# A one-core delta-rule and gated feed-forward kernel: another hand-kept order of all its work, 94 steps given to another engine or taken back, and nine filler products in place of five

## The chip, the cores and the metric

The kernel runs on one core of a Trainium2 chip. The metric is device microseconds of that core for one execution; smaller is better. The names used here are those of the profile: PE is TensorE, DVE is VectorE, ACT is ScalarE, POOL is GpSimd, and SP is SyncE, whose queue issues nearly all DMAs.

## The reference

Two blocks follow each other. The first runs over 768 positions for each of 4 batches and 8 heads; the second takes its output, token by token, through two matrix products with a gate between them.

```python
for t in range(S):                       # B, H, S, D = 4, 8, 768, 48
    kt, vt, bt = (k_n[:, :, t], v[:, :, t], beta[:, :, t, None])
    y[:, :, t] = np.einsum('bhd,bhde->bhe', q[:, :, t], state)
    v_old = np.einsum('bhde,bhd->bhe', state, kt)
    state = state + bt[:, :, :, None] * np.einsum('bhd,bhe->bhde', kt, vt - v_old)
...
h = x @ w_in                             # x: 3072 tokens of 384; w_in 384 x 2048
g = h * np.cos(h)
return (g @ w_out).astype(np.float32)    # w_out 2048 x 384
```

## The kernel before

**The first block** is cut into 24 units of 32 positions, and two units form a pair. For every unit PE forms the products of keys and queries with the keys (`gram`, L625), reads the state (`state`, L834), solves a triangular system by multiplying with an inverse that lies ready (`solve`, L897), updates the state (`update`, L920) and forms the output (`within`, L937; `features`, L956). DVE and ACT carry the results from one of these steps to the next.

**The inverse** of units 0 to 3 is made by row elimination on DVE and POOL (L727, L734, with products at L707). From unit 4 on it is made by POOL for a whole pair at once, and this is the path that the prediction follows. DVE writes the scaled products (`gram_keys`, L639). SP's queue puts them into device memory (`gram_put`, L766) and fetches them in another layout (`gram_get`, L775, tile `gb`). POOL inverts them in seven steps of a few columns each (`inv`, L797 and L804; 62 instructions for a pair). SP's queue puts the result out (`put`, L808) and fetches it for each unit of the pair (`get`, L817, four DMAs, tile `zt`). Only then can `solve` of that unit run. There is one buffer for `gb` and one for the matrix that is being inverted, so `gram_get` of a pair waits for the end of the inverse of the pair before it.

**The second block** works on pairs of units (256 tokens). The first two pairs form their hidden values with plain products (`hidden`, L980), the others with 20 block products and sums in place of 24 (`layer`, L1158; the sums over the inputs are `x_sum`, L1073, and those over the weights `in_sums`, L1116 and L1120). The gate is taken by ACT and DVE (`turns`, `rest`, `cos`, `gate`, L1021 to L1040). The output of the first pair is plain (L1181), that of the others takes seven products of half-size blocks in place of eight (`product`, L1246), with sums over the gated values (`left`, L1262) and over the weights (`right`, L1275), and collecting steps (L1298). The weights arrive in 28 pieces at the start; each is unpacked by ACT (`split`, L497 and L499), DVE (`shift`, L503 and L508) and POOL (`add`, L512).

**The order** is not found by a scheduler when the kernel is built. All work is registered as some 2,150 named steps with what they depend on. `Order.LINE` is a written list of their numbers, and `Order.run` issues them in just that order; each engine then works through its own instructions in this order and never takes a later one first. A step waits for what it depends on, and everything behind it on the same engine waits with it. Some steps may go to either of two engines: those listed in `Order.OTHER` go to the second one (for `left`, `right`, `weigh` and a few others POOL in place of DVE, for `x_sum` DVE in place of POOL, for `fold` and `unfold` ACT in place of DVE).

**Constant products** (`heat`, L1194) multiply a constant by itself into the output bank, and nothing reads the result. They are further work for PE in places where it has little. `HEAT` lists their widths. Before the change there are five, and the first output product (L1181) is registered as depending on all of them.

Of the kernel before, what the change touches and what calls it, by code (L numbers as in the profile page):

```python
# [46 lines left out]
HEAT = (512, 256, 256, 512, 128,)  # L47


class Order:  # L50

    OTHER = {
        ('weigh', 0, 0), ('unfold', 0), ('weigh', 0, 1), ('fold', 1), ('unfold', 1),
        ('weigh', 1, 0), ('fold', 2), ('weigh', 1, 1), ('unfold', 2), ('unfold', 3),
        ('right', 4, 0), ('left', 1, 2, 0), ('x_sum', 2, 'd'), ('x_sum', 2, 'n'),
        ('x_sum', 2, 'm'), ('x_sum', 2, 'e'), ('x_sum', 2, 'k'), ('x_sum', 2, 'g'),
        ('x_sum', 2, 'i'), ('x_sum', 2, 'l'), ('x_sum', 2, 'f'), ('x_sum', 2, 'h'),
        ('x_sum', 2, 'b0'), ('left', 2, 2, 0), ('x_sum', 3, 'd'), ('x_sum', 3, 'n'),
        ('x_sum', 3, 'm'), ('x_sum', 3, 'e'), ('x_sum', 3, 'k'), ('x_sum', 3, 'g'),
        ('x_sum', 3, 'i'), ('x_sum', 3, 'l'), ('x_sum', 3, 'f'), ('x_sum', 3, 'h'),  # L60
        ('x_sum', 3, 'b0'), ('left', 3, 1, 0), ('left', 3, 4, 1), ('left', 3, 3, 0),
        ('x_sum', 4, 'd'), ('x_sum', 4, 'n'), ('x_sum', 4, 'm'), ('x_sum', 4, 'e'),
        ('x_sum', 4, 'k'), ('x_sum', 4, 'g'), ('x_sum', 4, 'l'), ('x_sum', 4, 'f'),
        ('x_sum', 4, 'h'), ('x_sum', 4, 'b0'), ('left', 4, 4, 0), ('left', 4, 3, 0),
        ('left', 4, 3, 1), ('x_sum', 5, 'd'), ('x_sum', 5, 'm'), ('x_sum', 5, 'e'),
        ('x_sum', 5, 'i'), ('x_sum', 5, 'f'), ('x_sum', 5, 'h'), ('left', 5, 2, 0),
        ('left', 5, 4, 0), ('left', 5, 4, 1), ('left', 5, 3, 0), ('x_sum', 6, 'd'),
        ('x_sum', 6, 'e'), ('x_sum', 6, 'l'), ('x_sum', 6, 'f'), ('x_sum', 6, 'h'),
        ('x_sum', 6, 'b0'), ('left', 6, 2, 1), ('left', 6, 4, 0), ('left', 6, 3, 0),
        ('x_sum', 7, 'd'), ('x_sum', 7, 'n'), ('x_sum', 7, 'm'), ('x_sum', 7, 'g'),  # L70
        ('x_sum', 7, 'i'), ('x_sum', 7, 'h'), ('left', 7, 1, 0), ('left', 7, 2, 0),
        ('left', 7, 2, 1), ('left', 7, 4, 0), ('left', 7, 3, 1), ('x_sum', 8, 'd'),
        ('x_sum', 8, 'm'), ('x_sum', 8, 'e'), ('x_sum', 8, 'k'), ('x_sum', 8, 'f'),
        ('x_sum', 8, 'h'), ('x_sum', 8, 'b0'), ('left', 8, 4, 1), ('left', 8, 3, 0),
        ('x_sum', 9, 'n'), ('x_sum', 9, 'e'), ('x_sum', 9, 'k'), ('x_sum', 9, 'i'),
        ('x_sum', 9, 'b0'), ('left', 9, 2, 0), ('left', 9, 1, 1), ('left', 9, 4, 0),
        ('left', 9, 4, 1), ('left', 9, 3, 0), ('left', 9, 3, 1), ('x_sum', 10, 'd'),
        ('x_sum', 10, 'n'), ('x_sum', 10, 'e'), ('x_sum', 10, 'g'), ('x_sum', 10, 'l'),
        ('x_sum', 10, 'f'), ('x_sum', 10, 'h'), ('x_sum', 10, 'b0'), ('left', 10, 1, 0),
        ('left', 10, 1, 1), ('left', 10, 4, 0), ('left', 10, 3, 0), ('x_sum', 11, 'f'),  # L80
        ('x_sum', 11, 'b0'), ('left', 11, 1, 0), ('left', 11, 2, 0), ('left', 11, 2, 1),
        ('left', 11, 4, 0), ('left', 11, 4, 1),
# [139 lines left out]
def kernel(  # L222
# [1084 lines left out]
    def store(p, i, cols=slice(0, DM)):  # L1307
# [12 lines left out]
            x=2, x_sum=XS, turns=2, g=GATES, o=2, o_out=2,  # L1320
# [507 lines left out]
```

## Time and profile before

| what | value |
|---|---|
| three runs | 643.1, 647.96 and 650.33 us, median 647.96 |
| the profiled execution | 644.59 us, with a span of 642.8 us |
| PE | 613.6 us busy (95%) |
| DVE | 505.4 us busy (79%) |
| POOL | 447.9 us busy (70%) |
| ACT | 263.3 us busy (41%) |
| granted TensorE clock, mean | 0.981 |
| DMA | 50.01 MB, mean 78 GB/s |

The span is the time from the first to the last instruction of the program. Busy time counts overlapping instructions of one engine once. A row of the timeline gives start, length, engine, line, operation and, in brackets, how long the engine stood idle ahead of it and what ended that. PE works through its products one behind the other, so that a wait shows only where its whole queue ran dry.

### The profile page before, as it was taken

To read this page: it belongs to the slowest core of one execution; us is meant where nothing else is said; L and a number is where in the kernel's file an instruction comes from. 1 tells how busy PE (TensorE), PEld (TensorE's weight loads), DVE (VectorE), ACT (ScalarE), POOL (GpSimd) and SP (SyncE) were. 2 spreads that over 40 slices of the span, in tenths; PEclk is the share of its full clock that TensorE was granted. 3 is DMA by queue.
4 is the path that set the end of the run, shared out by engine and by line. 5 is a ranking of instruction groups with operands and counts; after the bars stand their busy time and mean duration, and the time that the engine had idled before them with its cause. 6 is when DMAs were issued, how large, how long until landed. Compare 5 with 4: busy or idle time off the path is not lost.

```text
span 642.8 us, 28246 instructions
## 1 busy us (share of the span) xinstructions
PE 613.6 (95%) x12316; PEld 572.7 (89%) x12316; DVE 505.4 (79%) x955; ACT 263.3 (41%) x467; POOL 447.9 (70%) x783
## 2 busy tenths in 40 slices
PE   5677999999999999999998999999999999999997
PEld 4566888886999989999998999999999999999997
DVE  7896887599999888789788778777778867556582
ACT  3535565822233631533523533622633433435340
POOL 4465899888888788787888886885897874152032
PEclk9677999999999999999999999999999999999999
DMA  6884475554453542635535404425304202000000
GB/s 122 217 215 133 102 197 140 123 93 70 75 96 51 100 76 40 115 64 99 89 42 98 86 7 84 74 53 101 67 2 85 51 2 34 28 2 26 2 25 25
DMA packets 202924, 50.01 MB, mean 78 GB/s; under 512 B 194544, under 2 KB 197760, under 8 KB 202800
## 3 DMA queue, kind: packets, MB, share of 16 engines
q1 hardware_dynamic: 201536, 47.82, 37.5%
q8 instruction: 97, 1.59, 1.1%
q10 hardware_dynamic: 1088, 0.20, 0.2%
q0 software_dynamic: 176, 0.18, 0.2%
q14 instruction: 27, 0.22, 0.1%
HBM read 38.19 MB, written 9.96 MB: 75 GB/s over the span
## 4 chain that ended last, share of the span: by engine, by line
PE 87%; DVE 7%; DMA 1%; issue 1%; POOL 1%; ACT 1%; SPq 0%; DVEq 0%; POOLq 0%
PE p_out L1246 29%; PE p_h L1158 28%; PE p_h L980 7%; PE p_kq L834 4%; PE p_out L1181 3%; PE p_u L897 3%; PE p_g L625 3%; PE p_s L920 3%; PE p_kq L937 3%; PE p_o L1246 2%; PE p_z L956 1%; DVE rows L734 1%; PE p_t L594 1%; DVE rows L727 1%; DVE g_ffn L1175 1%
## 5 line engine op out<-in xcount | busy, mean ns | idle before, releaser
L797 POOL TENSOR_TENSOR part<-z,gb 128x126 f32<-128x126 f32 (+22 forms) x310 | 138.8, 448 | 39.9 <-DMA gb<-g_dr 7.9
L804 POOL TENSOR_TENSOR z<-z,part 128x126 f32<-128x126 f32 (+22 forms) x310 | 145.8, 470 | 24.3
L1246 PE MATMUL p_out<-w_out,g_ffn 128*128 128x192 f32 x672 | 121.6, 329 | 2.0 <-DVE o L1298 1.8
L1246 PEld LDWEIGHTS p_out<-w_out,g_ffn 128*128 128x128 f32 x672 | 107.8, 190 | 3.7 <-issue 2.2
L1037 ACT ACTIVATE turns<-turns,halfpi 128x512 f32<-128x512 f32 x96 | 68.4, 720 | 78.7 <-DVE turns L1028 78.3
L1262 POOL TENSOR_TENSOR g_ffn<-g_ffn 128x512 f32<-128x512 f32 x37 | 49.0, 1329 | 67.3 <-DVE g_ffn L1040 46.0
L1246 PE MATMUL p_out<-w_sum,g_ffn 128*128 128x192 f32 x496 | 90.1, 329 | 0.4 <-DVE o L1298 0.4
L1158 PE MATMUL p_h<-x_sum,w_in 128*128 128x128 f32 x640 | 83.0, 277 | 0.3 <-DVE g_ffn L1175 0.3
L1246 PEld LDWEIGHTS p_out<-w_sum,g_ffn 128*128 128x128 f32 x496 | 79.5, 190 | 1.4 <-DVE o L1298 0.6
L1158 PEld LDWEIGHTS p_h<-x_sum,w_in 128*128 128x128 f32 x640 | 77.8, 192 | 1.7 <-DVE g_ffn L1175 0.6
L1021 ACT ACTIVATE turns<-g_ffn,quarter_turn 128x512 int32<-128x512 f32 x70 | 49.2, 719 | 59.8 <-DVE g_ffn L1175 38.9
L1175 DVE TENSOR_TENSOR g_ffn<-g_ffn,p_h 128x512 f32<-128x512 f32 x80 | 54.1, 679 | 24.6 <-PE p_h L1158 23.6
L1028 DVE SCALAR_TENSOR_TENSOR turns<-g_ffn,turns 128x512 f32<-128x512 f32 x70 | 55.8, 805 | 15.1 <-ACT turns L1021 14.9
L1040 DVE TENSOR_TENSOR g_ffn<-turns,g_ffn 128x512 f32<-128x512 f32 x70 | 50.9, 736 | 12.7 <-ACT turns L1037 12.6
L1158 PE MATMUL p_h<-x_sum,in_sum 128*128 128x128 f32 x400 | 54.0, 278 | 0.3 <-issue 0.3
L1158 PEld LDWEIGHTS p_h<-x_sum,in_sum 128*128 128x128 f32 x400 | 49.3, 191 | 1.5 <-issue 0.4
L980 PE MATMUL p_h<-x_ffn,w_in 128*128 128x128 f32 x384 | 48.3, 285 | 0.0
L980 PEld LDWEIGHTS p_h<-x_ffn,w_in 128*128 128x128 f32 x384 | 45.7, 198 | 1.0 <-issue 0.2
L1262 DVE TENSOR_TENSOR g_ffn<-g_ffn 128x512 f32<-128x512 f32 x51 | 44.3, 872 | 1.6 <-PE p_out L1246 1.5
L541 POOL TENSOR_TENSOR knrm<-ksum,halves 128x16 f32<-128x16 f32 (+1 forms) x14 | 38.8, 2768 | 9.0 <-DVE ksum L529 7.9
L1298 DVE SCALAR_TENSOR_TENSOR o<-p_out,o 128x192 f32<-128x192 f32 x74 | 25.0, 350 | 24.5 <-PE p_out L1246 23.8
L1170 ACT COPY p_h<-p_h 128x512 f32<-128x512 f32 x40 | 23.0, 574 | 48.9 <-PE p_h L1158 33.6
(145 smaller groups left out, 1052.9 us busy)
## 6 DMA issues: line engine op xcount, KB each, us to landing
gb<-g_dr SPq DMA_DIRECT2D x20, 256.0 KB, 4.1
vp<-in_v_dram SPq DMA_DIRECT2D x96, 48.0 KB, 3.0
in_sum<-in_moe_w_out_dram SPq DMA_DIRECT2D x12, 384.0 KB, 3.3
out_dram<-o SPq DMA_DIRECT2D x23, 192.0 KB, 2.5
in_sum<-in_moe_w_in_dram SPq DMA_DIRECT2D x8, 512.0 KB, 5.3
kp<-in_k_dram SPq DMA_DIRECT2D x128, 24.0 KB, 2.2
z_dr<-z SPq DMA_DIRECT2D x10, 256.0 KB, 3.6
zt<-z_dr SPq DMA_DIRECT2D x80, 32.0 KB, 2.4
```

The source lines that it names most:

```text
L541: nc.gpsimd.tensor_tensor(out=scales[m][2][:, part], in0=sums[m, part.start][:, 0:n], in1=halves[:, 0:n], op=ALU.pow,)
L797: nc.gpsimd.tensor_tensor(out=part, in0=z[:, 0:rows, j, None].to_broadcast(shape), in1=a[:, j, None, j + 1 :].to_broadcast(shape), op=ALU. ...
L804: nc.gpsimd.tensor_tensor(out=behind, in0=behind, in1=part, op=ALU.subtract)
L980: nc.tensor.matmul(p_h[:, i], w_in[:, t, (4 * k + i) * 128 : (4 * k + i + 1) * 128], xts[p][:, t, unit * 128 : (unit + 1) * 128], start=(i ...
L1021: nc.scalar.activation(turns[p, f], hidden_of(p, f), AF.Identity, bias=quarter_turn, scale=TURN)
L1028: nc.vector.scalar_tensor_tensor(out=r, in0=hidden_of(p, f), scalar=TURN, in1=t, op0=ALU.mult, op1=ALU.subtract,)
L1037: nc.scalar.activation(r, r, AF.Sin, bias=halfpi, scale=2.0 * math.pi)
L1040: nc.vector.tensor_tensor(out=place(p, f), in0=step_of(rests.pop((p, f)), f), in1=step_of(hidden_of(p, f), f), op=ALU.mult,)
L1158: nc.tensor.matmul(p_h[:, e], in_block(*w)[:, e], x_of(p, b), start=new and e == 0, stop=True, skip_group_check=True,)
L1175: nc.vector.tensor_tensor(out=part_of(p, to), in0=part_of(p, one), in1=part_of(p, two), op=op)
L1246: nc.tensor.matmul(p_o, left(p, part, a)[:, e % 4], right(e, b), start=(e == 0), stop=(e == FT // 2 - 1), skip_group_check=True,)
L1262: either(("left", p, x, s), nc.vector, nc.gpsimd).tensor_tensor(out=left(p, s, to), in0=left(p, s, one), in1=left(p, s, two), op=op)
```

## The change

Three things are edited, and nothing that is computed for the output changes.

- `LINE` is another permutation of the same steps, with four numbers more for the new constant products. Every engine's queue has another order, SP's included.
- `OTHER` differs in 94 steps: 25 `left` sums go from POOL to DVE and 16 from DVE to POOL; 22 `x_sum` sums go each way; 3 `weigh` products go from POOL to DVE; 3 `right` sums go from DVE to POOL and 1 back; 1 `fold` goes from DVE to ACT and 1 `unfold` from ACT to DVE.
- `HEAT` has nine widths (2,816 columns in all) in place of five (1,664), and the first output product is no longer registered as depending on them.

```diff
-HEAT = (512, 256, 256, 512, 128,)
+HEAT = (256, 128, 256, 512, 128, 256, 512, 512, 256,)
...
     OTHER = {
-        ('weigh', 0, 0), ('unfold', 0), ('weigh', 0, 1), ('fold', 1), ('unfold', 1),
...
+        ('weigh', 0, 0), ('unfold', 0), ('fold', 1), ('unfold', 1), ('fold', 2), ('fold', 3),
...
     LINE = """
-92 0 1 2 21 15 3 16 9 54 2143 10 11 17 55 18 93 123 2031 124 2035 14 4 60 56 57 6 22 2039 95 23 61
...
+0 15 16 9 1 21 17 2031 2 11 2035 3 2143 2039 22 14 18 54 4 6 7 5 23 55 19 92 56 60 24 25 2032 57
...
                 if last:
                     deps.append(last)
-                else:
-                    deps += [("heat", x) for x in range(len(HEAT))]
```

What the new order does to the queues that the prediction speaks of:

| queue | before | after |
|---|---|---|
| SP, first steps | k and q of units 2 and 3, then weight pieces between them | weight pieces 0 to 2, v of unit 0, k of unit 2, weight piece 3, q of unit 2 |
| DVE, ahead of the first elimination (L727) | no weight piece | weight pieces 0, 1 and 2 |
| PE, ahead of the first `hidden` product | both `gram` of units 2 and 3 | `gram` of unit 2 alone; eight of the nine constant products |
| POOL, inside the inverse of the first pair | weight pieces 14 to 21 | weight pieces 15 to 21 and 24, one `right` |
| SP, at the end of the inverse of units 6 and 7 | `put`, `gram_get`, `get` of unit 6 | `put`, `gram_put` of unit 9, `get` of unit 6, `gram_get` |
| SP, at the end of the inverse of units 16 and 17 | `put`, `gram_get`, `get`, `get` | `put`, `get` of unit 16, `gram_get` |
| SP, at the end of the inverse of units 20 and 21 | `put`, `gram_get`, a load, a store, a load, `get`, `get` | `put`, two `gram_put`, `get`, a store, `get`, `gram_get` |

More of the change, by code (lines that the diff above doesn't have):

```diff
@@ L44, in _consts @@
     ).astype(np.float32)
-HEAT = (512, 256, 256, 512, 128,)
+HEAT = (256, 128, 256, 512, 128, 256, 512, 512, 256,)
 class Order:
     OTHER = {
-        ('weigh', 0, 0), ('unfold', 0), ('weigh', 0, 1), ('fold', 1), ('unfold', 1),
[L54 to L61, printed above, removed]
-        ('x_sum', 4, 'd'), ('x_sum', 4, 'n'), ('x_sum', 4, 'm'), ('x_sum', 4, 'e'),
[L63 to L82, printed above, removed]
@@ new lines @@
+        ('weigh', 0, 0), ('unfold', 0), ('fold', 1), ('unfold', 1), ('fold', 2), ('fold', 3),
+        ('unfold', 2), ('right', 1, 2), ('right', 3, 2), ('right', 3, 6), ('left', 1, 1, 0),
+        ('left', 1, 4, 0), ('left', 1, 4, 1), ('x_sum', 2, 'd'), ('x_sum', 2, 'n'),
+        ('x_sum', 2, 'e'), ('x_sum', 2, 'k'), ('x_sum', 2, 'g'), ('x_sum', 2, 'i'),
+        ('x_sum', 2, 'l'), ('x_sum', 2, 'f'), ('x_sum', 2, 'h'), ('left', 2, 4, 0),
+        ('x_sum', 3, 'd'), ('x_sum', 3, 'n'), ('x_sum', 3, 'm'), ('x_sum', 3, 'e'),
@@ new lines @@
+        ('x_sum', 3, 'k'), ('x_sum', 3, 'g'), ('x_sum', 3, 'i'), ('x_sum', 3, 'l'),
+        ('x_sum', 3, 'f'), ('x_sum', 3, 'h'), ('left', 3, 1, 0), ('left', 3, 3, 1),
+        ('x_sum', 4, 'd'), ('x_sum', 4, 'n'), ('x_sum', 4, 'm'), ('x_sum', 4, 'e'),
+        ('x_sum', 4, 'k'), ('x_sum', 4, 'l'), ('x_sum', 4, 'f'), ('x_sum', 4, 'h'),
+        ('x_sum', 4, 'b0'), ('left', 4, 4, 0), ('x_sum', 5, 'd'), ('x_sum', 5, 'm'),
+        ('x_sum', 5, 'k'), ('x_sum', 5, 'g'), ('x_sum', 5, 'i'), ('x_sum', 5, 'l'),
@@ new lines @@
+        ('x_sum', 5, 'h'), ('x_sum', 5, 'b0'), ('left', 5, 1, 0), ('left', 5, 4, 1),
+        ('left', 5, 3, 1), ('x_sum', 6, 'n'), ('x_sum', 6, 'm'), ('x_sum', 6, 'e'),
+        ('x_sum', 6, 'i'), ('x_sum', 6, 'l'), ('x_sum', 6, 'f'), ('x_sum', 6, 'h'),
+        ('left', 6, 2, 0), ('x_sum', 7, 'd'), ('x_sum', 7, 'e'), ('x_sum', 7, 'i'),
+        ('x_sum', 7, 'f'), ('x_sum', 7, 'h'), ('x_sum', 7, 'b0'), ('left', 7, 1, 0),
+        ('x_sum', 8, 'd'), ('x_sum', 8, 'n'), ('x_sum', 8, 'k'), ('x_sum', 8, 'g'),
@@ new lines @@
+        ('x_sum', 8, 'l'), ('x_sum', 8, 'f'), ('x_sum', 8, 'h'), ('left', 8, 2, 0),
+        ('left', 8, 2, 1), ('left', 8, 3, 0), ('left', 8, 3, 1), ('x_sum', 9, 'm'),
+        ('x_sum', 9, 'l'), ('x_sum', 9, 'h'), ('x_sum', 9, 'b0'), ('left', 9, 1, 1),
+        ('left', 9, 2, 1), ('left', 9, 4, 0), ('left', 9, 3, 1), ('x_sum', 10, 'd'),
+        ('x_sum', 10, 'n'), ('x_sum', 10, 'm'), ('x_sum', 10, 'e'), ('x_sum', 10, 'k'),
+        ('x_sum', 10, 'l'), ('x_sum', 10, 'f'), ('x_sum', 10, 'b0'), ('left', 10, 1, 0),
@@ L83 @@
+        ('left', 10, 4, 1), ('left', 10, 3, 0), ('x_sum', 11, 'n'), ('x_sum', 11, 'k'),
+        ('x_sum', 11, 'i'), ('x_sum', 11, 'h'), ('left', 11, 1, 0), ('left', 11, 1, 1),
+        ('left', 11, 4, 1), ('left', 11, 3, 0), ('left', 11, 3, 1),
     }
     LINE = """
[98 rows of a table removed]
[98 rows of a table added]
 """
```

194 rows, old and new, of the table LINE are left out of this document.

## The prediction

> **What bounds the kernel now.** I read the page first: busy shares, slices and granted clock.
>
> ```profile
> span 642.8 us, 28246 instructions
> ...
> PE 613.6 (95%) x12316; PEld 572.7 (89%) x12316; DVE 505.4 (79%) x955; ACT 263.3 (41%) x467; POOL 447.9 (70%) x783
> ...
> DVE  7896887599999888789788778777778867556582
> ...
> PEclk9677999999999999999999999999999999999999
> ```
>
> PE is busy for 95% of the span and the clock is low only in the first tenth. So I read the busy time by stages (columns: stretch, its length, then PE, PEld, DVE, ACT, POOL; then granted clock, DMA share, GB/s).
>
> ```profile
> 0.00:20.00 20.00, 12.48 (x188) 9.97 (x188) 15.51 (x52) 7.83 (x15) 6.79 (x12) 1.00 0.73 145
> 20.00:60.00 40.00, 28.02 (x691) 23.60 (x691) 33.82 (x86) 16.64 (x35) 22.37 (x18) 0.70 0.77 203
> 60.00:160.00 100.00, 97.37 (x2377) 82.60 (x2376) 84.38 (x145) 54.15 (x106) 86.83 (x152) 1.00 0.52 116
> 160.00:320.00 160.00, 159.15 (x3633) 151.19 (x3633) 141.16 (x264) 62.48 (x109) 131.80 (x255) 1.00 0.47 81
> ```
>
> PE is idle for 7.5 + 12.0 = 19.5 us before 60, for 2.6 us from 60 to 160, and for some 3.5 us in small pieces from 160 to 600 (the longest 1.8). After its last product 3.3 us of collecting and storing remain. No order can win more than these 29 us and what the low clock costs. The waits of PE say who holds the head: DVE.
>
> ```profile
> PE p_g L625 <- DVE rows L727: 4.3, 1, 4.3
> PE p_u L897 <- DVE u_half L882: 3.6, 1, 3.6
> ```
>
> Part of why DVE is late there shows in the timeline of DVE and POOL: a sum of 8 columns, 0.17 us elsewhere, takes 1.27 us while POOL adds weights.
>
> ```profile
> 29.47 3.75 POOL L512 TENSOR_TENSOR w_in<-w_in,in_sum 128x512 uint32<-128x512 uint32 x3
> 29.50 1.27 DVE L552 TENSOR_TENSOR knrm<-knrm,tiny 128x8 f32<-128x8 f32 x1
> ```
>
> A PE with almost no idle time may still have a second bound just below it. So I followed one inverse from POOL to the solve that uses it (SP, POOL and PE timelines; units 8 to 10).
>
> ```profile
> 216.60 1.11 SPq L808 DMA_DIRECT2D z_dr<-z  x1
> 218.64 1.14 SPq L775 DMA_DIRECT2D gb<-g_dr  x2
> 220.57 1.81 SPq L817 DMA_DIRECT2D zt<-z_dr  x4
> ...
> 223.86 0.50 POOL L797 TENSOR_TENSOR part<-z,gb 128x31 f32<-128x31 f32 x1 [2.28 <-DMA gb<-g_dr]
> ...
> 225.93 0.80 PE L897 MATMUL p_u<-rhs,zt 32*32 32x48 f32 x64
> ```
>
> The inverse ends at 216.5. Its `put` goes out, `gram_get` of the next pair 2.1 us after the end, `get` of unit 8 4.0 us after `put`. zt lands at 224.6 and PE solves at 225.9. The same readings for units 6, 10, 12, 16, 18 and 22 leave 0.5 to 1.4 us between the landing of zt and the solve; unit 14 has 3.0, unit 4 has 3.5. POOL needs 33.5 us for an inverse with nothing else in it and 7.3 us to the start of the next, so 40.8 us for a pair, and here PE's work for a pair is about as long. So POOL's inverses are a second bound that ends only a microsecond before PE's queue gets there.
>
> **The change, part by part.**
>
> Constant products. 1,152 more columns; a 512-wide one takes 1.13 to 1.91 us (its two rows), so 2.5 to 4.3 us of PE. They stand in the head, where PE is idle for 12 of 40 us from 20 on; cost nothing. Without that cover it is those 2.5 to 4.3. What they could win is the clock:
>
> ```profile
> 25.00:30.00 5.00, 4.00 (x130) 3.16 (x130) 3.67 (x11) 3.17 (x7) 3.62 (x3) 0.50 0.93 242
> ```
>
> At half clock the three triangular products of unit 0 took 1.50 us (0.88 later), the update 1.56 (0.89), the first hidden product 4.66 (2.84): 3 x 0.62 + 0.67 + 1.82 = 4.4 us. PE waits for DVE in between, so I take 0 of it and keep both ends, 4.4 less and 4.3 more. The row shows PE busy for 4.0 of 5 us at half clock; the Trainium skill ("TensorE: Matmul & The Clock Gate", Part 1: The HAM clock gate) says that about 3.4 us of sustained work bring the full clock back. By that rule the five products that now stand together would do it, and the sum would be up to 4.4 us lower.
>
> Steps to other engines. DVE gets 25 - 16 = 9 `left` at 0.87, 3 `weigh` (between 0.54 of a `right` and 0.87; I take 0.6), loses 2 `right` at 0.58: +8.5 us. POOL loses 9 x 1.33 + 3 x 0.94 and gets 2 x 1.45: -11.9. Both stay below PE (80% and 68%), so only places matter, below.
>
> The head. DVE's first elimination starts at 15.6 now. With weight pieces 0 to 2 ahead of it (3.3 us of DVE) and k of unit 2 behind 1.5 MB on SP, I count 19.5. From there to the products of unit 3 the new queue holds 31.9 us of DVE work without the stretching by POOL; the old one got 27.1 such us done in 36 us. At that rate the `gram` of unit 3 comes at 58 to 62, not at 51.6, but one hidden product (2.9) is done ahead of it and 7.6 us more of DVE work are behind it. By the time the fifth unit's `gram` and the hidden products after it run (72.5 now) this leaves PE 0.5 to 5 us late. I take 2, nearer to the low end because much of the weights' work has been done by then.
>
> The inverses, each step against the one before:
> - Units 4, 5: 48 us of PE work lie ahead of the second `gram` in both orders, so the start moves as the head does, +2 (0 to 5). Inside, 9.9 us of other POOL work in place of 8.4: +1.5. End +3.5.
> - Units 6, 7: the old gap of 12.0 us came from a late `gram_keys`. It now has 6.9 us more DVE work ahead, but the inverse before it ends later too. I take 10 (8.5, nothing but POOL's own steps, to 12): -2.0; inside +0.6. Sum +2.1.
> - Units 8, 9: `get` of unit 6 now stands ahead of `gram_get` on SP. It waits 4.0 us for `put` and takes 1.8 to issue, so `gram_get` goes out 3.9 us later than the 2.1 above. Gap 6.9 becomes 10.8, and POOL's 9.1 us of other steps fit in it: +3.9; one `right` inside, +1.5. Sum +7.5.
> - Units 10, 11: one `left` inside, +1.3. Sum +8.8. The solve of unit 10 has 0.5 us of slack and 3.0 us more PE work ahead of it (all `layer` and `product` steps at their means), so PE waits till it is 5.3 us late.
> - Later pairs move by -1.3, -1.2, 0, +0.8, -4.6 and, where both `get` go ahead of `gram_get` (4.0 + 1.8 + 0.6 + 1.8 against 0.6), +7.0: sums 7.5, 6.3, 6.3, 7.1, 2.5, 9.5. With each solve's slack and place, PE is 4.4, 5.7, 3.6, 5.8 late and, at unit 22, 5.5. I take 5.5.
>
> The rest. PE goes 91 times from wide to narrow products in place of 88; a block product takes 1.50 behind a narrow one and 1.30 behind another: +0.6. Of the 3.5 us that PE waits after 160, about half vanishes where it now waits for zt: -1.8. The end stays: 3.3 us after the last product.
>
> Sum: 644.6 (the profiled execution: span 642.8 and 1.8 around it) + 5.5 + 0.6 - 1.8 = 648.9. The median of the runs shown lies 3.4 above the profiled one, so **652.3**. Its own bounds: an inverse without stretching saves 3 us twice, the head costs 0 and the gap is 8.5, then PE is held by nothing and 644 remains; head +5, gap 12 and none of the 1.8 back give 660.
>
> **The rivals.**
>
> (1) Faster: VectorE and GpSimd stand less in each other's way. In the first 60 us stretched instructions cost DVE 8.3 us (2.9 in the L552 to L557 of unit 3, 2.2 in two weight pieces, 3.2 in eliminations and a spread), and the inverses of units 6 to 9 take 36.1 and 36.5 where 33.5 is possible. If the new places avoid this, the first inverse starts 4 us early instead of 2 late and two inverses end 5.6 sooner: 5.5 - 6 - 5.6 = -6.1, so 644.6 - 6.1 + 0.6 - 1.8 + 3.4 = 640.7. Against it: POOL adds more weights in a row while DVE eliminates. It decides if the first inverse starts before 87 and the next two take under 34.
>
> (2) Slower still: DVE does not catch up. 6.9 us more DVE work ahead of `gram_keys` of unit 7, in a stage where DVE is 84% busy and 98% soon after. Then that inverse starts 8.9 us late in place of 1.5, PE is 12.9 late and the time is 644.6 + 12.9 + 0.6 + 3.4 = 661.5.
>
> (3) The later fetch is hidden anyway: POOL has 9.1 us of its own steps in the gap and stretched inverses have room, PE alone decides: 644.6 + 0.6 - 1.8 + 3.4 = 646.8.
>
> (4) The clock is full from 30 on, and unit 0 hangs on PE's products, not on DVE: 652.3 - 4.4 = 647.9. For it: five constant products in one place. Against it: PE was busy for 4.0 of 5 us at half clock in the row above.
>
> **How the numbers follow.** Forecast 0.35, (1) 0.27, (2) 0.20, (3) 0.11, (4) 0.07. One per cent (6.5 us) is about what a measurement of this kernel tells from no change. Under 641.5: 0.25 from (1), 0.02 from (3). Over 654.4: 0.20 from (2), 0.13 from the forecast's upper part. The rest, 0.40, lies within. The likeliest case's own range is 644 to 660; the range for 8 in 10 leaves out the outer part of (1) and (2): 638 to 662.
>
> **What would show it.** Right: `gb` of units 8 and 9 issued some 6 us behind the end of the inverse before it, solves of units 8 and 10 with PE idle in front, ended by zt, and the first hidden product near 52. Wrong: no idle PE there, POOL never waiting for gb, or DVE's small sums at 0.17 us throughout the head.

## The result and the profile after

The changed kernel takes 649.98 us (median of 20 runs, 647.3 to 653.02), the kernel before 645.1 us (20 runs, 642.58 to 650.33). The ratio is 1.0071 with a 95% interval of 1.005 to 1.0093. The changed kernel is 4.6 us slower by the ratio and 4.9 us by the medians, less than the one per cent that the prediction counted as no change. The profiled execution took 651.29 us with a span of 649.4. The median of 647.96 that the prediction worked from came from three runs and was 2.9 us too high.

The page of the changed kernel, the lines that answer to those shown of before:

```profile
span 649.4 us, 28232 instructions
...
PE 621.2 (96%) x12324; PEld 579.3 (89%) x12324; DVE 498.4 (77%) x966; ACT 265.8 (41%) x466; POOL 428.9 (66%) x773
...
PEclk9978999999999999899999999999999999999999
```

PE is busy 7.6 us longer for nearly the same products (four more constant ones), and the clock row begins 9 9 7 8 where it began 9 6 7 7. Two of the stages shown of before (stretch, length, PE, PEld, DVE, ACT, POOL, granted clock, DMA share, GB/s):

```profile
20.00:60.00 40.00, 32.45 (x658) 27.35 (x657) 33.42 (x101) 18.50 (x37) 16.98 (x11) 0.87 0.78 188
...
160.00:320.00 160.00, 156.88 (x3413) 147.86 (x3412) 133.39 (x252) 59.47 (x101) 125.63 (x247) 0.99 0.47 78
```

From 160 to 320 PE stands idle for 3.1 us, where before it was 0.9. The waits of PE say what for (line, releaser: us in total, times, longest):

```profile
PE p_u L894 <- DVE u_half L879: 3.5, 2, 2.8
PE p_h L1155 <- ACT p_h L1167: 2.8, 1, 2.8
```

The wait of 4.3 us for `rows` in front of `gram` of unit 3 is gone. A new one of 2.8 us stands in one place, in front of a layer product, and ACT ends it. No wait for zt is in the list.

**Where the time went.** I price each step of PE at the median of its kind over both traces (early steps at the smaller of their two durations) and take the work done by a time from that time; what is left is lost time. The working is an estimate from the two traces. The difference to before in us:

| at (us) | 30 | 60 | 80 | 120 | 140 | 200 | 260 | 280 | 340 | 400 | 460 | end |
|---|---|---|---|---|---|---|---|---|---|---|---|---|
| changed kernel | +3.8 | +2.6 | +1.9 | +4.8 | +1.9 | +4.2 | +4.2 | +8.8 | +9.8 | +7.0 | +5.4 | +6.6 |
| run e4, below | 0.0 | -1.4 | -1.1 | -1.2 | -1.2 | +0.7 | +0.6 | +1.9 | +4.4 | +2.3 | +1.3 | +1.8 |

So 4.2 us are lost up to 200, 4.6 in one place between 260 and 280, and some 2 are won back behind it, where before had waits of its own (1.82 us at 348, and several of 0.3). This is one profiled run each, 6.6 us apart; the medians are 4.9 us apart.

**The place at 267 us.** In what follows, inverse 5 is that of units 10 and 11, inverse 6 that of units 12 and 13, and so on; solve 10 is the `solve` of unit 10. The timeline of the changed kernel, all engines:

```profile
260.79 3.67 SPq L763 DMA_DIRECT2D g_dr<-g  x6
...
262.00 0.23 POOL L801 TENSOR_TENSOR z<-z,part 128x16 f32<-128x16 f32 x1
...
264.56 0.55 SPq L805 DMA_DIRECT2D z_dr<-z  x1
...
268.15 0.62 ACT L779 COPY z<-consts 128x512 f32<-128x512 f32 x1 [2.91 <-DMA z_dr<-z]
268.68 0.59 ACT L1169 ACTIVATE g_ffn<-p_h 128x512 f32<-128x512 f32 x1
269.30 0.57 ACT L1167 COPY p_h<-p_h 128x512 f32<-128x512 f32 x1
...
269.92 2.07 PE L1155 MATMUL p_h<-x_sum,in_sum 128*128 128x128 f32 x8 [2.75 <-ACT p_h L1167]
...
271.79 1.60 PE L1155 MATMUL p_h<-x_ffn,w_in 128*128 128x128 f32 x8
```

POOL ends inverse 5 at 262.2. Its `put` is not issued before 264.56, since SP works through six `gram_put` transfers ahead of it. There is one tile z, so ACT's copy of the identity for inverse 6 (`eye` 6, L779) waits 2.91 us until `put` has read it. Two layer copies stand behind it on ACT, and PE waits 2.75 us for the second. The two products behind it take 2.07 and 1.60 us; the third, at 273.23, takes 1.06. The windows around it show why:

```profile
268.00:269.00 1.00, 0.00 (x0) 0.00 (x0) 0.00 (x0) 0.84 (x2) 0.00 (x0) 1.00 1.16 324
...
270.00:271.00 1.00, 1.00 (x5) 1.00 (x6) 0.46 (x1) 0.51 (x1) 0.18 (x1) 0.50 1.05 210
...
273.00:274.00 1.00, 1.00 (x11) 1.00 (x10) 0.00 (x0) 0.52 (x1) 0.77 (x4) 1.00 0.39 70
```

The granted clock is 0.50 from about 269.5 to 272.9. Wait and half clock cost 4.4 us together.

### The profile page after: what moved, and what is told of

Its sections match the earlier page's. It is cut to its first block, busy times and chain, and to the rows that moved or that the text cites. A ratio compares the mean times of both kernels' runs of the same rounds, so it can differ in the third digit from the quotient of the medians.

```text
span 649.4 us, 28232 instructions
## 1 busy us (share of the span) xinstructions
PE 621.2 (96%) x12324; PEld 579.3 (89%) x12324; DVE 498.4 (77%) x966; ACT 265.8 (41%) x466; POOL 428.9 (66%) x773
## 4 chain that ended last, share of the span: by engine, by line
PE 81%; DMA 5%; DVE 4%; SPq 3%; POOL 2%; issue 2%; ACT 1%; DVEq 0%; ACTq 0%; POOLq 0%
PE p_out L1243 27%; PE p_h L1155 27%; PE p_h L977 6%; PE p_kq L831 4%; PE p_out L1178 3%; PE p_s L917 3%; PE p_u L894 3%; PE p_kq L934 2%; SPq L354 2%; PE p_g L622 2%; PE p_o L1243 2%; PE p_z L953 1%; DMA in_sum<-in_moe_w_in_dram 1%; DMA in_sum<-in_moe_w_out_dram 1%; DMA qp<-in_q_dram 1%
## 5 line engine op out<-in xcount | busy, mean ns | idle before, releaser
L794 POOL TENSOR_TENSOR part<-z,gb 128x126 f32<-128x126 f32 (+22 forms) x310 | 136.4, 440 | 61.4 <-ACT turns L1034 20.3
L801 POOL TENSOR_TENSOR z<-z,part 128x126 f32<-128x126 f32 (+22 forms) x310 | 143.1, 462 | 24.3
L1259 POOL TENSOR_TENSOR g_ffn<-g_ffn 128x512 f32<-128x512 f32 x28 | 37.6, 1348 | 58.5 <-DVE g_ffn L1259 26.0
L1037 DVE TENSOR_TENSOR g_ffn<-turns,g_ffn 128x512 f32<-128x512 f32 x70 | 55.2, 797 | 10.9 <-ACT turns L1034 10.9
L1025 DVE SCALAR_TENSOR_TENSOR turns<-g_ffn,turns 128x512 f32<-128x512 f32 x70 | 51.4, 739 | 12.6 <-ACT turns L1018 12.3
L1259 DVE TENSOR_TENSOR g_ffn<-g_ffn 128x512 f32<-128x512 f32 x60 | 46.0, 771 | 4.3 <-PE p_out L1243 4.2
L977 PE MATMUL p_h<-x_ffn,w_in 128*128 128x128 f32 x384 | 48.5, 285 | 0.5 <-ACT row_copies L715 0.3
L538 POOL TENSOR_TENSOR knrm<-ksum,halves 128x16 f32<-128x16 f32 (+1 forms) x14 | 38.0, 2715 | 13.0 <-DVE rows L724 5.7
L1155 PE MATMUL p_h<-x_ffn,w_in 128*128 128x128 f32 x320 | 43.3, 280 | 0.0
```

The source lines that it names most:

```text
L538: nc.gpsimd.tensor_tensor(out=scales[m][2][:, part], in0=sums[m, part.start][:, 0:n], in1=halves[:, 0:n], op=ALU.pow,)
L794: nc.gpsimd.tensor_tensor(out=part, in0=z[:, 0:rows, j, None].to_broadcast(shape), in1=a[:, j, None, j + 1 :].to_broadcast(shape), op=ALU. ...
L801: nc.gpsimd.tensor_tensor(out=behind, in0=behind, in1=part, op=ALU.subtract)
L977: nc.tensor.matmul(p_h[:, i], w_in[:, t, (4 * k + i) * 128 : (4 * k + i + 1) * 128], xts[p][:, t, unit * 128 : (unit + 1) * 128], start=(i ...
L1025: nc.vector.scalar_tensor_tensor(out=r, in0=hidden_of(p, f), scalar=TURN, in1=t, op0=ALU.mult, op1=ALU.subtract,)
L1037: nc.vector.tensor_tensor(out=place(p, f), in0=step_of(rests.pop((p, f)), f), in1=step_of(hidden_of(p, f), f), op=ALU.mult,)
```

## The experiments

The ratios below are to the kernel before, run beside each of these runs on the same chip; 95% intervals stand in brackets. In the runs that keep the changed kernel's order on PE, the start of the same product can be compared straight away. In us against the changed kernel's own trace (minus is earlier):

| run | at 235 | at 273 | at 317 | at 334 | at 358 | end of PE |
|---|---|---|---|---|---|---|
| e1, `eye` 6 later | -1.0 | -5.5 | -5.0 | -1.8 | -1.1 | -0.6 |
| e2, `gram_get` first | +0.9 | -1.6 | -1.6 | -1.6 | -0.9 | 0.0 |
| e8, `eye` 6 and `scale` 8 later | -1.9 | -6.3 | -6.3 | -2.5 | -2.0 | -1.9 |
| e10, `put` 5 first | -0.2 | -4.6 | +0.2 | -0.1 | +0.6 | +0.3 |
| e11, e8 and the store ahead | -0.3 | -4.7 | -4.6 | -5.7 | -3.7 | -3.3 |

The first 100 us alone differ by up to 3 us from run to run of one order (e12 below), so the steps between two columns say more than a column.

### e1: the identity copy behind the two layer copies

```diff
 LINE (names for the numbers)
-eye 6, ..., layer_out 4 3, ..., layer_out 4 7
+..., layer_out 4 3, ..., layer_out 4 7, eye 6
```

> The changed kernel with one ScalarE step moved: the copy that lays out the identity for inverse 6 (`eye` 6) stands behind the two layer copies that were queued behind it. Theory S (the stall at 267 us is time lost on the path of TensorE): the wait of 2.75 us in front of the layer product and the half clock behind it (products of 2.07 and 1.60 us where 0.9 is usual) go away, and nothing later takes them back: 4.4 us less than the changed kernel, about 645.5. Theory Z (the forecast's: the chain of inverses sets the pace): the stall goes, but solve 12 stood at 316.5 with its zt landed at 314.6 and solve 14 at 357.3 with its zt landed at 356.9, so TensorE arrives early and waits there for zt by up to 4 us: no more than 0.5 to 1 us less in all, about 649, with a new wait of 3 to 4 us in front of solve 14.

652.51 us (10 runs), ratio to before 1.0095 (1.0066 to 1.0125). The stall at 267 is gone, and PE gains the 4.4 us there that were expected. It keeps them up to 326 and then loses 3.2:

```profile
326.03 0.39 DVE L549 TENSOR_TENSOR knrm<-knrm,tiny 128x16 f32<-128x16 f32 x1 [2.81 <-POOL knrm L538]
...
327.04 0.68 DVE L1172 TENSOR_TENSOR g_ffn<-g_ffn,p_h 128x512 f32<-128x512 f32 x1
...
327.77 1.44 PE L1155 MATMUL p_h<-x_ffn,in_sum 128*128 128x128 f32 x8 [1.96 <-DVE g_ffn L1172]
```

The line at 326.03 is DVE's: the first of four steps of `scale` 8 waits 2.81 us for the norms that POOL makes (L538, 3.38 us long) between two parts of inverse 7. Behind these four stands the add that PE wants. The changed kernel has the same wait with 0.78 us on PE, since it comes 5 us later. Theory S said that nothing takes the gain back: wrong. Theory Z named zt of solve 14 as the taker: it takes 0.6, but the larger part goes to a step that has nothing to do with zt. What the two share is POOL. By the table nothing of the 4.4 us is left at the end: PE was 1.0 us ahead before the stall and is 0.6 ahead at its last product.

### e2: gram_get ahead of the fetches

```diff
 LINE, SP's part
-get 6, gram_get 4
+gram_get 4, get 6
...
-get 16, gram_get 9
+gram_get 9, get 16
...
-get 21, store 7 0, get 20, gram_get 11
+gram_get 11, get 21, store 7 0, get 20
```

> The changed kernel with SyncE's order of before at three pairs: gram_get 4, 9 and 11 stand ahead of the zt fetches that were put ahead of them. Theory Z: inverse 4 starts about 3.9 us earlier (gap of 10.6 us down to about 6.9), the later inverses keep 2 to 4 us of that, TensorE is released earlier and the time falls by 4 us, to about 646. Theory S: inverse 4 starts as much earlier, but no solve of the changed kernel has idle TensorE ended by zt in front of it, so the time stays within 0.5 us of the changed kernel's 650; only the slack between landing and solve grows, by 2 to 4 us.

651.6 us (12 runs), 1.008 (1.0046 to 1.0113). Inverse 4 starts 10.3 us behind the end of inverse 3; in the changed kernel that was 10.6, and 6.9 was expected. SP's queue of the changed kernel, and then that of this run with the solve of unit 6:

```profile
174.45 0.38 SPq L805 DMA_DIRECT2D z_dr<-z  x1
174.93 2.83 SPq L763 DMA_DIRECT2D g_dr<-g  x3
177.90 1.99 SPq L814 DMA_DIRECT2D zt<-z_dr  x4
180.00 1.13 SPq L772 DMA_DIRECT2D gb<-g_dr  x2
```

```profile
174.30 3.29 SPq L763 DMA_DIRECT2D g_dr<-g  x3
179.11 1.13 SPq L772 DMA_DIRECT2D gb<-g_dr  x2
180.33 2.01 SPq L814 DMA_DIRECT2D zt<-z_dr  x4
...
184.41 1.41 PE L894 MATMUL p_u<-rhs,zt 32*32 32x48 f32 x64 [1.19 <-DMA zt<-z_dr]
```

`gram_put` of unit 9 is what stands between `put` and `gram_get`: it takes some 3 us to issue, and without the fetch in between `gram_get` waits another 1.5 us behind it. The fetch filled that time. POOL would not have been free much earlier either, as its rows in the changed kernel show:

```profile
182.74 1.27 POOL L1259 TENSOR_TENSOR g_ffn<-g_ffn 128x512 f32<-128x512 f32 x1
184.99 0.24 POOL L794 TENSOR_TENSOR part<-z,gb 128x31 f32<-128x31 f32 x1 [0.98 <-DMA gb<-g_dr]
```

Its own steps last until 184.0, 9.6 us behind the end of inverse 3, and it waits 0.98 us for gb. So an earlier `gram_get` could win 1 us here at most. At the two later pairs the move does shorten the gap: inverse 9 starts 9.7 us behind the end of inverse 8 in place of 13.7, inverse 11 starts 11.7 us behind that of inverse 10 in place of 16.5. But these inverses then take 3.5 and 5.5 us longer, and inverse 11 ends at 544.1 in both traces.

Moved back, the fetch lets solve 6 wait 1.19 us for zt. At 267 the wait is 1.56 us in place of 2.75 and no half clock follows, which is worth 2.5 us; the end is the same. Both theories had the gap ahead of inverse 4 shrink by 3.9 us, which fails. That the time stays the same speaks for S. The smaller wait at 267 is no sign of an earlier chain: `put` 5 goes out at 264.40 (264.56 in the changed kernel) and the layer product behind the wait starts at 269.74 (269.92), but PE arrives 1.0 us later.

### e12: both edits

> Both edits at once, the identity copy of inverse 6 behind the two layer copies and gram_get 4, 9 and 11 ahead of the zt fetches. Theory S: the same as the first alone, about 645.5. Theory Z: 4 us less from the second, and the first is now free to give its 4.4 us as well: about 642. A mixture (the chain takes back what the first edit gives, unless the second makes room): the first alone 648 to 649, the second alone 650, both together 645.

654.52 us (6 runs), 1.0108 (1.0058 to 1.0157). None of the three theories had this. The trace is late at the start: at 12.6 PE waits 4.04 us for the turned keys (2.40 in the changed kernel, with the same queues up to there). At 60 it has caught up, and at 100 it is 2.3 us behind, after a granted clock of 0.50 from 93.9 to 97.3. The stall at 267 is gone, that of `scale` 8 is 1.96 us. It tells nothing more than e1 and e2 do.

### e3 to e6: which stretch costs the time

```diff
 LINE, OTHER, HEAT
-the changed kernel's, all of it
+e3: steps 1 to 485 as before (about 165 us), the rest as in the changed kernel
+e4: steps 1 to 694 as before (about 215 us), the rest as in the changed kernel
+e5: steps 1 to 694 as in the changed kernel, the rest as before
+e6: steps 1 to 944 as before (about 285 us), the rest as in the changed kernel
```

> The first 490 steps (up to about 165 us) in the order of before, with its engines and its five constant products, the rest in the order of the changed kernel. Theory S (the head and the chains of units 2 and 3 cost the changed kernel 4.2 us, the stall at 267 another 4.4, and before's own later stalls gave 4.3 back): about 4 us less than the changed kernel, 645 to 646, with the stall near 263 still there. Theory Z (the inverses of pairs 4 and 5 set the time, and their steps stand in the part that stays): within 1.5 us of the changed kernel, 648.5 to 650.

653.04 us (6 runs), 1.012 (1.0071 to 1.0168). Inconclusive, by my seam: DVE's sums over the weights, left over from the one order, stand ahead of `solve_out` of unit 5, and PE waits 5.84 us for u at 158.5. Up to 150 the trace is within 1 us of before. The 490 in the expectation counts the five constant products.

> Up to the 694th step (about 215 us, where the two orders differ by five steps and one product) the order, engines and five constant products of before, from there the order and engines of the changed kernel. Theory L (lateness is won and lost in stretches and carried on: the first 215 us cost the changed kernel 4.2 us, what lies behind them 2.4): 4 us less than the changed kernel and 2.4 more than before, with a stall near 263 as in the changed kernel. Theory F (another engine stands a few us behind TensorE everywhere, so a lead is taken back, as the lead of 4.4 us was when the copy for inverse 6 was moved): within 1.5 us of the changed kernel, 4 to 5 more than before, with new waits of TensorE for VectorE or zt behind 260.

647.41 us (12 runs) against 647.91 of before on the same chip: 0.999 (0.9967 to 1.0013), 5.2 us less than the changed kernel. The seam is clean. The changed kernel's own order behind 215 costs nothing against before that the times show, and its stall has shrunk:

```profile
258.36 0.23 POOL L801 TENSOR_TENSOR z<-z,part 128x16 f32<-128x16 f32 x1
258.61 0.36 SPq L805 DMA_DIRECT2D z_dr<-z  x1
...
262.26 0.62 ACT L779 COPY z<-consts 128x512 f32<-128x512 f32 x1 [0.66 <-DMA z_dr<-z]
...
264.03 1.16 PE L1155 MATMUL p_h<-x_sum,in_sum 128*128 128x128 f32 x8 [0.64 <-ACT p_h L1167]
```

Inverse 5 ends 3.6 us earlier than in the changed kernel, the `gram_put` transfers are out before it ends, `put` follows at once, and PE waits 0.64 us. So the stall at 267 does not come from the order there alone: with the same order it shrinks from 2.75 to 0.64 us when what lies before 215 is on time.

> The mirror: up to the same 694th step the order, engines and nine constant products of the changed kernel, from there before's order and engines. Theory L: before plus 4.2 us. Theory F (lateness is taken back by the slack of the later part, since TensorE is late there and no longer meets the waits that before has at 348 us): before plus 2 us or less.

659.11 us (6 runs), 1.0158 (1.0129 to 1.0188). Both expectations were too low. Up to the seam the lateness is +3.4 us against before. By the starts of the same products PE is 11.5 us behind before at 240, so the seam itself costs some 8:

```profile
217.89 0.55 POOL L801 TENSOR_TENSOR z<-z,part 128x16 f32<-128x16 f32 x1
...
223.22 3.71 SPq L354 DMA_DIRECT2D kp<-in_k_dram  x8
227.02 1.69 SPq L763 DMA_DIRECT2D g_dr<-g  x3
228.82 0.54 SPq L805 DMA_DIRECT2D z_dr<-z  x1
...
232.31 0.62 ACT L779 COPY z<-consts 128x512 f32<-128x512 f32 x1 [6.07 <-DMA z_dr<-z]
...
234.92 0.68 DVE L1172 TENSOR_TENSOR g_ffn<-p_h,g_ffn 128x512 f32<-128x512 f32 x1
...
235.74 1.42 PE L894 MATMUL p_u<-rhs,zt 32*32 32x48 f32 x64 [6.38 <-DVE g_ffn L1172]
```

Loads that one order has later and the other earlier meet on SP ahead of `gram_put` 11 and `put` 4. `put` goes out 10.4 us behind the end of its inverse, and the place at 267 is repeated in large: the identity copy for inverse 5 waits 6.07 us on ACT, the gate steps queued behind it come late, DVE's add behind those ends at 235.6, and PE goes on at 235.74 after 6.38 us of idle. The fetch of zt, issued at 232.25, lands at 236.2 with its last part, so it would have held solve 8 about as long. This is no clean mirror of e4, but it prices a late `put`, and both of its ways to PE.

> Up to the 944th step (about 285 us, behind the place where the changed kernel stalls) the order of before, then that of the changed kernel. Theory L: TensorE was 8.8 us behind before at 280 and 6.6 at the end, so the changed kernel's last part is 2.2 us cheaper than before's: before minus 2 us, about 7 less than the changed kernel. Theory F: before plus 0 to 2 us, with TensorE waiting near 330 for VectorE, which waits for the norms of pair 8 on GpSimd, as in the run with the later copy.

648.24 us (12 runs), 1.0005 (0.9982 to 1.0028). The cheaper last part of theory L does not show; PE waits 2.1 us at the seam for an add, 0.78 at 327 for ACT's copy into an output tile and 0.78 at 353 for zt. Theory F had the time right; the wait for VectorE near 330 that it named is not there.

### e7: no constant products

```diff
-HEAT = (256, 128, 256, 512, 128, 256, 512, 512, 256,)
+HEAT = ()
 LINE: without their nine numbers
```

> The changed kernel without its nine constant products (their results are not used). Price theory: they lie in idle time, so the time is the same. Clock theory (they shorten the half clock of the first 60 us, which took 10.2 us with nine and 23.9 us with five in the kernel before): the half clock lasts 20 to 25 us and the time is 1 to 3 us longer than the changed kernel's. Opposite theory: the products themselves stand in the way of rows and transposes, and the time is 1 to 3 us shorter.

656.34 us (6 runs), 1.0115 (1.0086 to 1.0144): by the ratios 2.8 us more than the changed kernel, with intervals that just overlap. The clock row of this run says 1.00 up to 55, against what I expected, but the products themselves tell another speed. The changed kernel, then this run:

```profile
21.93 1.09 PE L591 MATMUL p_t<-consts,kp 128*128 128x128 f32 x4
...
27.48 3.90 PE L1191 MATMUL p_out<-halfpi 128*128 128x128 f32 x10
31.21 0.60 PE L591 MATMUL p_t<-consts,kp 128*128 128x128 f32 x4
...
34.05 0.88 PE L861 MATMUL p_w<-vp,halves_z 32*32 32x48 f32 x64
```

```profile
30.05 1.09 PE L591 MATMUL p_t<-consts,qp 128*128 128x128 f32 x4 [1.38 <-DMA qp<-in_q_dram]
...
33.87 1.50 PE L861 MATMUL p_w<-vp,halves_z 32*32 32x48 f32 x64 [1.12 <-issue]
...
45.45 1.11 PE L591 MATMUL p_t<-consts,kp 128*128 128x128 f32 x4
```

Four transposes take 1.09 us at 21.93 and 0.60 at 31.21, right behind five constant products of 3.9 us in one piece; the triangular product behind them takes 0.88 us. Without the constant products the transposes still take 1.09 at 30 and 1.11 at 45, and the triangular products 1.50. So the products are followed by full speed from 31 to 40, where this run is at half. (From 41.7 to 46 both are at half.) But this is not what makes the 2.8 us. At 60 the run without the products is 1.8 us ahead; the same product in the changed kernel, then in this run:

```profile
60.07 0.88 PE L861 MATMUL p_w<-rhs,halves_z 32*32 32x48 f32 x64 [0.94 <-ACT rows L649]
```

```profile
58.30 1.21 PE L861 MATMUL p_w<-rhs,halves_z 32*32 32x48 f32 x49 [0.94 <-ACT rows L649]
```

It loses 3.7 us by 66: PE waits 1.03 us at 59.5, and its granted clock is 0.50 from 58.2 to 65.0 (1.00 in the changed kernel from 57.9 on). Between 91 and 96 it loses 2.2, at half clock once more. Whether the products prevent these two stretches or the traces differ there by chance is not shown by one trace of each.

### e8 to e11: the give-backs, one by one

```diff
 LINE
+e8: as e1, and scale 8 behind layer_out 5 14, 5 16, 5 18
+e9: as e4, with the two moves of e8
+e10: put 5 ahead of gram_put 12 and 13, nothing else
+e11: as e8, and k 19 behind store 3 0
```

> The changed kernel with the identity copy of inverse 6 behind the two layer copies, as before, and VectorE's four steps of `scale` 8 moved behind the three layer adds that were queued behind them (in the run with the later copy they waited 2.81 us for GpSimd's norms of pair 8, which stand behind a part of inverse 7 there, and TensorE waited 1.96 us for an add behind them and ran at half clock after it: 3.2 us given back at 326 to 334). Theory W (each give-back is a queue's order, and goes when the order does): the stall near 326 goes, and of the 5.5 us that TensorE was ahead of the changed kernel at 273 some 4 to 5 are still there at 340; at solve 14 zt takes 1 to 2 of them; the time is 3 to 4 us less than the changed kernel, some 646. Theory F (GpSimd's chain gives the pace, whichever step passes it on): zt of solve 14 holds TensorE at 352 to 356 by what was gained, and the time is within 1 us of the changed kernel.

647.79 us (12 runs), 1.0045 (1.0019 to 1.0071). The wait for the add is gone and PE is 7.2 us ahead of the changed kernel at its next product; then it loses 4.7 in the same microseconds, for a third reason:

```profile
314.98 10.82 SPq L354 DMA_DIRECT2D kp<-in_k_dram  x16
...
325.90 0.60 SPq L1307 DMA_DIRECT2D out_dram<-o  x1
...
328.31 0.33 ACT L1282 ACTIVATE o<-p_out 128x192 f32<-128x192 f32 x1 [6.22 <-DMA out_dram<-o]
...
328.69 2.85 PE L1243 MATMUL p_out<-w_out,g_ffn 128*128 128x192 f32 x8 [3.29 <-ACT o L1282]
```

SP has 16 key loads ahead of the store of an output tile, ACT's copy into that tile waits 6.22 us for the store, and PE 3.29 us for the copy. Theory W holds for its own stall and fails for the sum; zt of solve 14 took little.

> Before's order up to the 694th step, the changed kernel's behind it (the run that came out at 0.999 of before), with the same two moves, the identity copy of inverse 6 and `scale` 8 behind what they held up. That run's trace shows a wait of 0.64 us at 263 and one of 2.11 us at 324 (with no half clock). Theory W: both go, about 2.5 us less than that run, 0.995 of before. Theory F: zt of solve 14, which stood 0.5 us ahead there, takes most of it: 0.997 to 1.0 of before.

645.93 us (12 runs), 1.0001 (0.9976 to 1.0026). Both waits (0.64 and 2.11 us) are gone from the trace, which ends 0.8 us ahead of e4's and 1.0 behind that of before; the times don't tell the three apart. Theory F's 0.997 to 1.0 is nearest.

> The changed kernel with one SyncE step moved: the transfer of inverse 5 to memory (`put` 5) stands ahead of gram_put 12 and 13 (six transfers, 3.67 us of issue), behind which it was issued at 264.56 although the inverse ended at 262.2. If that order is what held the identity copy: the put is issued near 262.4, the copy on ScalarE waits less than 1 us, the stall of 2.75 us at 267 and the half clock behind it are gone, and the trace is 4.4 us ahead at 273, as with the later copy; the price is gram_put 12 and 13 about 1.7 us later and gb of inverse 6 some 0.6 to 1.7 us later, so that norms 8 and zt of solve 14 come that much later, and more is given back at 326 and 356: in all within 1 us of the changed kernel. If something else held the copy (the landing itself), the stall stays above 2 us.

652.58 us (6 runs), 1.0104 (1.007 to 1.0137). `put` goes out at 261.61, right at the end of its inverse, the copy of the identity does not wait, and the stall of 267 is gone: SP's order was its cause here, together with what is late before 215, since the same order makes 0.64 us in e4. But the `gram_put` transfers now come later, and everything behind them on SP with them:

```profile
261.61 0.39 SPq L805 DMA_DIRECT2D z_dr<-z  x1
262.09 4.35 SPq L763 DMA_DIRECT2D g_dr<-g  x6
...
267.99 1.14 SPq L772 DMA_DIRECT2D gb<-g_dr  x2
...
269.81 2.92 SPq L814 DMA_DIRECT2D zt<-z_dr  x4
...
274.13 1.25 PE L894 MATMUL p_u<-rhs,zt 32*32 32x48 f32 x64 [3.13 <-DMA zt<-z_dr]
```

zt for solve 10 is fetched at 269.81, 1.7 us later than in the changed kernel, and PE, 4.6 us earlier there, waits 3.13 us for it and then runs at half clock. Within the three products behind the solve all is given back.

> The run with the identity copy of inverse 6 and `scale` 8 moved, and one SyncE step more: the second key load (`k` 19, eight transfers) stands behind the store of an output tile (`store` 3, 0) that it was ahead of. In that run the store was issued at 325.90 behind 10.82 us of key loads, ScalarE's copy into the tile waited 6.22 us for it, and TensorE waited 3.29 us for the copy. With the move the store is issued near 320.5 and the copy waits less than 1 us. Theory W (each give-back is one queue's order): the stall of 3.29 us and the half clock behind it are gone, TensorE is some 6 us ahead of the changed kernel at 340, and 4 us at the end: about 645 to 646, 1.000 of before. Theory F (the chain of inverses stands close behind TensorE whatever is mended): put 7 was issued at 348.5 there and its zt cannot be back before some 353 to 355, so solve 14, which would come at 351, waits there for what was gained, and the end is 2 to 2.5 us ahead of the changed kernel: about 648, 1.003 to 1.004 of before.

649.17 us (12 runs), 1.0041 (1.0017 to 1.0066). The store goes out at 320.42 and the third give-back is gone; PE is 5.7 us ahead at 334. A wait of 0.94 us at 336 and zt at solve 14 (0.36 us of idle, and a solve of 1.26 us in place of 0.80) take 2, and 3.3 are left at the end of the trace. By the trace this is between theory W (4 us) and theory F (2 to 2.5); by the times (1.0071 against 1.0041, with overlapping intervals) the gain is 2 us and barely seen, and the ratio is the one that theory F gave.

## Why the prediction was right, and where it was right by accident

652.3 was forecast on a median of 647.96, so +4.3 us; measured were +4.9 us between the medians. The time lies 2.3 us below the forecast and inside its range of 638 to 662. The sum holds only in part, and that its total comes so near is in part luck.

- **The head: right.** The first elimination was put at 19.5 and starts at 20.02 (15.57 before), behind the weight pieces on DVE; `gram` of unit 3 was put at 58 to 62 and comes at 58.27; PE was to be 2 us late near 72.5, and the lost time is +1.9 at 80. That the steps up to 215 carry the result is shown by e4: with before's order there, the 4.6 us are gone.
- **The chain of inverses: late as forecast, but mostly by less, and the wait wrong.** Ends of the inverses against before, predicted and measured: units 4 and 5 +3.5 and +5.6; 6 and 7 +2.1 and +1.3; 8 and 9 +7.5 and +4.8; 10 and 11 +8.8 and +4.9; 12 and 13 +7.5 and +4.2; 14 and 15 +6.3 and +6.7; 16 and 17 +6.3 and +4.2; 18 and 19 +7.1 and +4.8; 20 and 21 +2.5 and +0.2; 22 and 23 +9.5 and +5.6. The gap ahead of units 8 and 9 was put at 10.8 and is 10.6. Its reason was wrong: the 3.9 us were charged to the fetch ahead of `gram_get`, but `gram_put` of unit 9 holds `gram_get` up about as long, and POOL's own steps fill 9.6 us of the gap (e2 moved the fetch and won 0.3).
- **The step that failed** is "PE waits till it is 5.3 us late" at solve 10, and with it the 5.5 in the sum. Solve 8 starts at 230.59 with the last part of its zt landing at 230.8, so the chain does touch PE there, but PE does not stand idle, since it is itself 4.2 us late by then. At solve 10 zt lands 3.5 us ahead. "No idle PE there" was one of the prediction's own signs of being wrong, and it came. The chain's lateness reaches PE by the tile z instead: 2.75 us of wait and 1.7 of half clock at 267. The prediction had followed z only from POOL to the solve, not back to the copy that needs it free and to what is queued behind that copy on ACT. Where the stall is taken away, zt comes close but does not always hold PE: in e1, e8 and e11 it lands 0.5 to 1.2 us ahead of solve 10 and PE does not wait; in e10, where the fetch itself goes out later, PE waits 3.13 us for it.
- **The late stalls: the size right.** 1.8 us were to vanish. Of PE's idle time between 320 and 480 (2.92 us before, 0.82 after) 2.1 did, but no wait for zt has taken its place, as the prediction had it. Before's rows give 3.8 us of idle PE from 160 to 600; the prediction read 3.5.
- **Constant products.** The prediction's 0 is for nine in place of five. No run isolates that: e7 compares nine with none, and 2.8 us is what all nine are worth by the times, with the cause open. What the five of before did shows in its trace, whose transposes take 0.63 us at 15.43; the changed kernel's still take 1.09 at 21.93. Rival (4) said full speed from 30 on, and from 31.2 it is there, up to 40.8. The Trainium skill ("TensorE: Matmul & The Clock Gate", Part 1: The HAM clock gate) says that about 3.4 us of sustained work bring it. The trace agrees with that behind the 3.9 us of constant products, but not ahead of them: PE works from 16.79 to 24.96 without a gap, and the transposes at 22.82 still take 1.06 us. The 647.9 of rival (4) did not come, because unit 0 hangs on DVE (the wait of 2.80 us for `u_half` in front of its last triangular product), as the prediction had it.
- **Busy times.** The sum had DVE 8.5 us busier and POOL 11.9 less; measured were 7.0 and 19.0 less. Both stay below PE, as it said.
- **The 3.4 us** between the profiled run and the median were no property of the kernel. With 20 runs before's median is 645.1, 0.5 above its profiled run; without that term the forecast would have been 649.4, nearer to what was measured.
- **The other rivals.** (1) asked for a first inverse before 87 and the next two under 34 us; it starts at 90.0, and they take 34.9 and 36.3. (2) asked for `gram_keys` of unit 7 to be 8.9 us late; the inverse that waits for it starts 2.5 late. (3) was right that the later fetch is hidden, and by the POOL steps that it named, but wrong about the time.

**What stays open.** Which of the steps before 215 makes the 4.2 us was not taken apart by a run: e4 puts back the order, the engines and the five constant products of before all at once. The traces show the first elimination 4.4 us late and the first inverse ending 5.6 late. Why e11, with three stalls mended, does not come out clearer in the times was not tried further.

## What to carry to other kernels

Here, with PE at 96%, other queues stood one to five us behind it. A stall that is removed is worth what the next dependency leaves: one move won 4.4 us on the spot and nothing at the end, because POOL's norms, a store behind 16 loads and a fetch were each waiting their turn. Look, for a transfer that frees a single buffer, at what is queued ahead of it on its issuing engine and at what is queued behind the step that needs the buffer. Before any of this is mended, ask how early the stage before it delivers: with the same order behind 215 us the kernel came out 5 us slower than before with one head and level with it with another.

## What the runs showed of the hardware

- **One short wait costs the clock too.** Behind waits of PE of 1.67 us (e3, at 243), 1.96 (e1), 2.08 (e6, at the seam), 2.75 (changed kernel), 3.13 (e10) and 3.29 (e8) the granted clock was 0.50 for some 3.4 us. In e7 it was so behind two waits of 1.00 and 0.65 at 94, and the hidden product there took 4.54 us in place of 2.94. Behind 1.82 (before, at 348), 2.09 and 2.11 (e4, at 163 and 324), 1.71 (e5, at 361) and 1.56 (e2) it stayed at 1.00. So from 1.7 to 2.1 us it went either way, and the same wait can cost 1.7 to 2 us more (changed kernel, e1) or nothing. The Trainium skill (the same page and section) has the clock fall after an idle window of about 3.4 us; here waits shorter than that were enough, and the measurement decides.
- **The clock row is not the whole speed.** In the first 30 us of the changed kernel the row says 1.00 while transposes take 1.09 us that take 0.60 later; in e7 this lasts to about 47 us. The duration of a known product is the better reading there.
- **Runs of one order differ early.** The wait for the turned keys of unit 1 at 12.6 us was 2.3 to 4.0 us in the eight runs that begin as the changed kernel does, and single waits of 1.4 to 2.1 us in front of `state` that nothing visible ends ("issue") come in some traces (e3 at 243, e4 at 163, e7 at 243, e9 at 236) and not in others.
